# Attention inside two mixed layers: row sums and norms issued behind the products with V, and a unit's additions placed behind the low part of a projection sum on VectorE

## The chip, the cores and the metric

The kernel runs on one core of a Trainium2 chip. The metric is the device time of one launch in microseconds (us). Three runs of the kernel before took 3855.62, 3857.41 and 3857.58 us, so the median is 3857.41 us.

## The reference

Four residual steps are computed on a sequence of 2048 rows with 1024 columns: attention, a spectral filter, attention, the spectral filter, each on the layer-normed input. The change touches attention alone, which has 32 heads of 32 columns.

```python
def _A_ref(x, wqkv, wo):
    B, S, D = x.shape
    H = 32
    Dh = D // H
    qkv = (lambda x, *d: x.transpose(*d))((x @ wqkv).reshape(B, S, 3, H, Dh), 2, 0, 3, 1, 4)
    q, k, v = qkv[0], qkv[1], qkv[2]
    scores = jnp.einsum("bhqd,bhkd->bhqk", q, k) * (Dh ** -0.5)
    p = _softmax(scores, axis=-1)
    o = jnp.einsum("bhqk,bhkd->bhqd", p, v)
    return (lambda x, *d: x.transpose(*d))(o, 0, 2, 1, 3).reshape(B, S, D) @ wo
...
x = A_x
x = x + _A_ref(_layernorm(x, axis=-1), A_wqkv, A_wo)
x = x + _B_ref(_layernorm(x, axis=-1), B_w_r, B_w_i)
x = x + _A_ref(_layernorm(x, axis=-1), A_wqkv, A_wo)
x = x + _B_ref(_layernorm(x, axis=-1), B_w_r, B_w_i)
```

## The kernel before

**Units.** Attention works on 8 groups `g` of 4 heads. In a group the 2048 query rows are cut into 4 chunks `c` of 512, and the 2048 keys into 16 tiles `kt` of 128. One step of the main loop, a *unit* (g, c, kt), is one key tile against one chunk of queries, so a layer has 512 units. The text writes S(n), add(n) and so on for key tile n of a chunk.

**What a unit issues.** `S` (L557) makes the scores: 12 TensorE matmuls (L563) that use 32 rows of the array each, into two PSUM tiles `s` of 1024 columns, followed by two exponentials on ScalarE (L567), which write the halves of `p`. `PV` (L569) multiplies `p` with V: matmuls in fp32 that use 32 columns of the array each (L573). They are issued for two units at once, at each even key tile. `add` (L580) adds the two halves of `p` into two running sums `acc` on VectorE, two instructions (L586; L584 at key tile 1, which adds the tiles 0 and 1). At key tile 0 there is nothing to add.

**Row sums.** After the last key tile of a chunk, `fin` (L588) sums `acc` over the partitions: four fp32 matmuls with a 128x32 block of ones (L592), 32 array columns each as in `PV`. Their output `z` takes a PSUM tile of the same pool as the scores (`psS`, 3 tiles in turn). VectorE transposes `z` (L593), inverts it (L595), and multiplies the product with V (L596 to L599). At key tile 5 of that next chunk `out` (L602) splits the result in a high and a low half: L605 on ScalarE, L606 on VectorE.

**The filler.** Behind the scores of each odd key tile, TensorE gets a piece of the next groups' projections (`filler`, L397, portioned by `slots`, L619). A projection sum for k or q (`qk_chunk`, L324) is 24 matmuls into a single PSUM tile `x` (`psX`, one buffer), portioned as 8+8+8 or 12+12. When it is done, `split` (L165) reads `x` twice: ScalarE writes the high fp16 part (L167), then VectorE the low part (L168), which needs the high one. The next sum's first matmul needs `x` back, that is, the low part done. VectorE also squares the high part (`sq`, L342). A group with even `g` has 12 such sums beside it (4 for each of k, q, k), a group with odd `g` 4 (q) and then 8 sums for v, which ScalarE alone empties; group 6 has 8 and then pieces of the output projection, group 7 only those. The projection weights of the next phase are split as well, by L167 and L168 on tiles `wqk` and `wv`; in the first layer alone, VectorE also takes their maxima (L259).

**Norms.** After the fourth sum of a k or q phase, `norms` (L349) sums the squares over each head: four bf16 matmuls with a 128x32 block (L355), 32 columns each, into a tile of `psS` again, which VectorE reduces to a maximum (L357, `mqk`). In the main loop there are 14 of these in a layer.

**What sets the order.** On TensorE and ScalarE the main loop's own order holds (`manual_schedule`, L633). On VectorE a scheduler places instructions by the program's order and by when it takes their inputs to be ready, when the kernel is built; on the chip each engine then works its list in that fixed order. At an even key tile n the loop issues S(n), the products of the units n-2 and n-1, and add(n-2); at the odd tile n+1 it issues S(n+1), add(n-1), and then the filler. The row sums stand at key tile 1 of the next chunk, behind add(15), and norms stand in `slots`, ahead of a filler piece.

## Time and profile before

| what | value |
|---|---|
| median of three runs | 3857.41 us |
| profiled execution, its own time | 3855.25 us |
| profiled execution, span of the trace | 3853.3 us |
| TensorE matmuls busy | 3720.5 us, 97% |
| VectorE busy | 3165.8 us, 82% |
| ScalarE busy | 2898.3 us, 75% |
| granted TensorE clock, mean | 0.99 |
| main attention loop, first layer (first to last scores) | 123.5 to 1624.1 us |
| main attention loop, second layer | 2046.8 to 3535.6 us |

The profile's page has the busy time of each engine, the chain of work that ended last, and the costliest groups of instructions. A group's row reads: line, engine, operation, out<-in, shapes, count, then busy time, mean of one in ns, and the idle time of the engine just before such instructions with what ended it. The timeline's rows read: start in us from the span's start, length in us, engine, line, operation, out<-in, shapes, count; equal neighbours are merged into one row, and in brackets stands the idle time ahead with what released it. The ends of matmuls are modelled, so that the text takes the cost of a group of matmuls from its start to the start of the next group.

### The profile page before, as it was taken

To read this page: it belongs to the slowest core of one execution; us is meant where nothing else is said; L and a number is where in the kernel's file an instruction comes from. 1 tells how busy PE (TensorE), PEld (TensorE's weight loads), DVE (VectorE), ACT (ScalarE), POOL (GpSimd) and SP (SyncE) were. 2 spreads that over 40 slices of the span, in tenths; PEclk is the share of its full clock that TensorE was granted. 3 is DMA by queue.
4 is the path that set the end of the run, shared out by engine and by line. 5 is a ranking of instruction groups with operands and counts; after the bars stand their busy time and mean duration, and the time that the engine had idled before them with its cause. 6 is when DMAs were issued, how large, how long until landed. Compare 5 with 4: busy or idle time off the path is not lost.

```text
span 3853.3 us, 79584 instructions
## 1 busy us (share of the span) xinstructions
PE 3720.5 (97%) x32951; PEld 1640.1 (43%) x32951; DVE 3165.8 (82%) x3869; ACT 2898.3 (75%) x3567; POOL 303.0 (8%) x386
## 2 busy tenths in 40 slices
PE   6999999999999999999989999999999999999998
PEld 4322433342234233378853334333423432333788
DVE  6699899889998988866666998899899889889554
ACT  4678887888788866667756888888888888666585
POOL 1000000000000000004320000000000000000143
PEclk9999999999999999999999999999999999999999
DMA  8000000000000221243270000000000002112433
GB/s 206 15 12 23 12 12 18 18 12 18 12 26 7 73 71 64 80 149 124 63 175 15 18 18 13 12 18 23 10 18 12 23 12 91 53 64 72 150 99 104
DMA packets 165573, 194.07 MB, mean 50 GB/s; under 512 B 74960, under 2 KB 120656, under 8 KB 164176
## 3 DMA queue, kind: packets, MB, share of 16 engines
q1 hardware_dynamic: 164912, 188.82, 15.9%
q8 instruction: 260, 4.26, 0.5%
q14 instruction: 113, 0.93, 0.1%
q10 hardware_dynamic: 288, 0.07, 0.0%
HBM read 123.83 MB, written 48.23 MB: 45 GB/s over the span
## 4 chain that ended last, share of the span: by engine, by line
PE 73%; DVE 12%; issue 8%; ACT 3%; DMA 2%; POOL 2%; SPq 0%; DVEq 0%; POOLq 0%; ACTq 0%
PE o L573 19%; PE s L563 16%; PE x L338 12%; PE x L382 7%; PE x L441 6%; DVE R L586 4%; PE s L441 2%; PE ps L861 2%; PE ps L801 2%; ACT p L567 1%; PE s L592 1%; PE ps L792 1%; DMA wst<-in_wp 1%; PE ps L976 1%; PE ps L930 1%
## 5 line engine op out<-in xcount | busy, mean ns | idle before, releaser
L567 ACT ACTIVATE p<-s,bias 128x1024 f32<-128x1024 f32 x2048 | 2167.8, 1111 | 553.5 <-PE s L563 542.6
L586 DVE TENSOR_TENSOR R<-R,p 128x1024 f32<-128x1024 f32 x1792 | 2085.4, 1219 | 111.2 <-ACT p L567 107.8
L573 PE MATMUL o<-p,R 128*32 128x512 f32 x8192 | 985.0, 598 | 0.0
L338 PE MATMUL x<-big,wqk 128*128 128x512 f16 x2880 | 682.7, 383 | 21.1 <-DVE Q L168 6.5
L563 PEld LDWEIGHTS <-R 32*128 32x128 f16 x12288 | 231.6, 92 | 760.3 <-issue 644.6
L338 PEld LDWEIGHTS <-wqk 128*128 128x128 f16 x3072 | 277.6, 98 | 458.5 <-issue 165.4
L563 PE MATMUL s<-R 32*128 32x512 f16 x6144 | 430.9, 378 | 10.6 <-ACT p L567 8.9
L573 PEld LDWEIGHTS o<-p,R 128*32 128x32 f32 x8192 | 213.7, 109 | 523.8 <-issue 523.8
L563 PE MATMUL s<-Q,R 32*128 32x512 f16 x6144 | 425.4, 378 | 7.5 <-DVE R L482 5.5
L382 PEld LDWEIGHTS <-big 128*128 128x128 f16 x3072 | 293.1, 99 | 144.3 <-issue 66.2
L382 PE MATMUL x<-wv,big 128*128 128x256 f16 x2688 | 320.5, 275 | 35.0 <-DMA big<-hl 35.0
L584 DVE SCALAR_TENSOR_TENSOR R<-p 128x1024 f32<-128x1024 f32 x128 | 153.8, 1203 | 198.9 <-ACT p L567 198.6
L441 PE MATMUL x<-big 128*128 128x512 f16 x1050 | 241.6, 380 | 0.0
L363 POOL PARTITION_ALL_REDUCE mall<-mqk x16 | 41.8, 2612 | 2325.5 <-DVE mqk L357 2313.9
L441 PEld LDWEIGHTS <-big 128*128 128x128 f16 x1344 | 124.3, 98 | 180.5 <-issue 42.7
L909 DVE TENSOR_TENSOR H<-G,H 128x512 f16<-128x512 f32 (+1 forms) x68 | 46.3, 680 | 113.1 <-ACT H L908 112.9
L861 PE MATMUL ps<-cbi,H 128*128 128x256 f16 (+1 forms) x792 | 100.5, 275 | 7.9 <-ACT H L908 6.2
L854 ACT COPY U<-ps 64x256 f32<-64x256 f32 (+1 forms) x272 | 97.0, 357 | 11.6 <-PE ps L861 6.4
L854 ACT COPY B<-ps 64x256 f32<-64x256 f32 (+1 forms) x272 | 97.0, 356 | 7.0 <-PE ps L861 2.8
L861 PE MATMUL ps<-cb,big 128*128 128x256 f16 x780 | 97.6, 275 | 0.0
L167 ACT ACTIVATE R<-x 128x512 f16<-128x512 f32 x88 | 52.6, 598 | 54.8 <-PE x L338 54.7
L806 DVE TENSOR_TENSOR big<-ps,big 128x512 f16<-128x512 f32 x64 | 44.4, 694 | 50.4 <-ACT big L805 50.3
(428 smaller groups left out, 2967.7 us busy)
## 6 DMA issues: line engine op xcount, KB each, us to landing
wst<-in_wp SPq DMA_DIRECT2D x96, 256.0 KB, 3.0
R<-y SPq DMA_DIRECT2D x32, 512.0 KB, 5.4
w<-in_w SPq DMA_DIRECT2D x60, 256.0 KB, 2.7
od<-ohl SPq DMA_DIRECT2D x56, 256.0 KB, 2.4
big<-od SPq DMA_DIRECT2D x16, 896.0 KB, 7.0
y<-R SPq DMA_DIRECT2D x20, 512.0 KB, 2.6
R<-in_x SPq DMA_DIRECT2D x16, 512.0 KB, 5.6
wst<-in_wo SPq DMA_DIRECT2D x32, 256.0 KB, 3.0
```

The source lines that it names most:

```text
L167: nc.scalar.activation(hi, src, AF.Copy, scale=scale)
L338: nc.tensor.matmul(ps, a, b, start=d == 0 and i == 0, stop=d == 7 and i == 2)
L382: nc.tensor.matmul(ps[:, j], l, r, start=d == 0 and i == 0, stop=d == 7 and i == 2)
L441: nc.tensor.matmul(p, a, b, start=start and d == ds[0] and i == 0, stop=stop and d == ds[-1] and i == 2)
L563: nc.tensor.matmul(s[h // 2][:, h % 2], K[g][r, a, kt * 128:kt * 128 + 128], Q[g][r, b, c * 512:c * 512 + 512], start=i == 0, stop=i == 2)
L567: nc.scalar.activation(p, s[hf], AF.Exp, bias=bias[g], scale=SCALE / (SQ * SQ))
L573: nc.tensor.matmul(O[g, c][32 * h:32 * h + 32], V[g][:, kt, 32 * h:32 * h + 32], P[g, c, kt, h // 2][:, h % 2], start=kt == 0, stop=kt == ...
L584: nc.vector.scalar_tensor_tensor(acc[hf], P[g, c, 0, hf], 1e-34, p, op0=ALU.add, op1=ALU.add)
L586: nc.vector.tensor_add(acc[hf], acc[hf], p)
L801: nc.tensor.matmul(pa[:, j], tt[:, j], mm[:, g], start=True, stop=True)
L854: nc.scalar.copy(ov[64 * r:64 * r + 64, a0:a0 + m, x], tl[64 * x:64 * x + 64, :m, r])
L861: nc.tensor.matmul(out, l, r, start=k == 0, stop=k == len(mm_) - 1)
```

## The change

Three things are moved; no instruction is added, removed or made otherwise.

1. At key tile 0 of a chunk, the loop issues the additions of both of the last units (tiles 14 and 15 of the chunk before) and the row sums `fin` at once, directly behind the products with V. `fin` stood one unit later, behind the scores of key tile 1.
2. `norms` is taken out of `slots`. It is called at key tiles 2, 6, 10 and 14, directly behind the products with V.
3. `split` returns the instruction of the low part, and `qk_chunk` keeps it in a list `lows`. At an odd key tile, if `lows` holds one, the additions of the pair's second unit are traced inside `tc.issue_after(...)`: on VectorE they must stand behind that low part. The low part is that of the sum that ended two units earlier, at the key tile of the very unit that is added.

```diff
@@ -1,5 +1,5 @@
 import numpy as np
-from contextlib import ExitStack
+from contextlib import ExitStack, nullcontext
 import concourse.bass as bass
 import concourse.tile as tile
 from concourse import mybir
@@ -165,7 +165,7 @@
 def split(nc, hi, lo, src, scale):
 
     nc.scalar.activation(hi, src, AF.Copy, scale=scale)
-    nc.vector.scalar_tensor_tensor(lo, src, scale, hi, op0=ALU.mult, op1=ALU.subtract)
+    return nc.vector.scalar_tensor_tensor(lo, src, scale, hi, op0=ALU.mult, op1=ALU.subtract)
 
 
 def run(g):
@@ -338,13 +338,13 @@
                 nc.tensor.matmul(ps, a, b, start=d == 0 and i == 0, stop=d == 7 and i == 2)
                 if d < 7 or i < 2:
                     yield
-        split(nc, t[:, 0], t[:, 1], ps, SQ / (SX * SW))
+        lows.append(split(nc, t[:, 0], t[:, 1], ps, SQ / (SX * SW)))
         (nc.gpsimd if both else nc.vector).tensor_tensor(nrm[ph][:, c], t[:, 0], t[:, 0], op=ALU.mult)
         if c == 3:
             left_norms.append(ph)
         yield
 
-    left_norms = []
+    left_norms, lows = [], []
 
     def norms():
         kind, g = ph = left_norms.pop(0)
@@ -609,6 +609,7 @@
         else:
             olast[c] = t
 
+    lows.clear()
     pend, done, late = [], [], []
     fill, lwo, wof = filler(), load_wo(), wo_parts()
     left, rests = 16, {}
@@ -622,8 +623,6 @@
             k = max(1, int(n / sums + 0.5))
             m = -(-steps // k)
             for i in range(0, steps, m):
-                while left_norms:
-                    norms()
                 for _ in range(min(m, steps - i)):
                     next(f, None)
                 n -= 1
@@ -643,11 +642,18 @@
                         PV(*w)
                     late = pend
                     pend = []
+                    if kt == 0 and late:
+                        for w in late:
+                            add(*w)
+                        done = [late[1][:2]]
+                        fin(*done[0])
+                        late = []
+                if kt % 4 == 2:
+                    while left_norms:
+                        norms()
                 for w in late[:1]:
-                    add(*w)
-                    if w[2] == NKT - 1:
-                        fin(*w[:2])
-                        done = [w[:2]]
+                    with tc.issue_after(lows.pop().ins) if kt % 2 and lows else nullcontext():
+                        add(*w)
                 late = late[1:]
                 if kt == 5 and done:
                     out(*done.pop())
```

The lists of TensorE, VectorE and the others that result are these. ScalarE, GpSimd and the DMA queue keep their order.

On VectorE, second layer, group 2, end of chunk 0. `L586` x2 is the additions of one unit, `R<-x,R` of L168 the low part of a projection sum, `sq` the square, `wqk` the low part of weights, L593 the transpose of the row sums. Before:

```order
L168 SCALAR_TENSOR_TENSOR R<-x,R 128x512
L342 TENSOR_TENSOR sq<-R 128x512
L586 TENSOR_TENSOR R<-R,p 128x1024 x12
L168 SCALAR_TENSOR_TENSOR R<-x,R 128x512
L342 TENSOR_TENSOR sq<-R 128x512
L586 TENSOR_TENSOR R<-R,p 128x1024 x4
L168 SCALAR_TENSOR_TENSOR wqk<-wst,wqk 128x512 x2
L586 TENSOR_TENSOR R<-R,p 128x1024 x4
L584 SCALAR_TENSOR_TENSOR R<-p 128x1024
L593 STREAM_TRANSPOSE zt<-s 128x512
L584 SCALAR_TENSOR_TENSOR R<-p 128x1024
```

With the change:

```order
L168 SCALAR_TENSOR_TENSOR R<-x,R 128x512
L342 TENSOR_TENSOR sq<-R 128x512
L586 TENSOR_TENSOR R<-R,p 128x1024 x12
L168 SCALAR_TENSOR_TENSOR R<-x,R 128x512
L342 TENSOR_TENSOR sq<-R 128x512
L586 TENSOR_TENSOR R<-R,p 128x1024 x6
L168 SCALAR_TENSOR_TENSOR wqk<-wst,wqk 128x512 x2
L586 TENSOR_TENSOR R<-R,p 128x1024 x4
L593 STREAM_TRANSPOSE zt<-s 128x512
L595 RECIPROCAL rc<-zt 128x16
L596 TENSOR_TENSOR fr<-fr,rc 128x16
```

The second low part has moved ahead of the additions of one unit: of those, x6 instead of x4 now stand between it and the weights' low parts. The additions of the sum's own key tile are behind it. The row sums' chain now stands ahead of L584, the next chunk's first additions, not among them.

On TensorE, second layer, the row sums of the same chunk (with the semaphores that an instruction waits for). Before, behind the last scores of key tile 1 and ahead of the filler:

```order
L563 MATMUL s<-R 128x512
L592 MATMUL s<-R,ones 32x512 [waits DVE_49,Activation_49]
L592 MATMUL s<-R,ones 32x512
L592 MATMUL s<-R,ones 32x512 [waits DVE_49]
L592 MATMUL s<-R,ones 32x512
L338 LDWEIGHTS wqk
L338 MATMUL x<-big,wqk 128x512
```

With the change, behind the products with V and ahead of the scores of key tile 1:

```order
L573 MATMUL o<-p,R 32x512 x6
L573 MATMUL o<-p,R 32x512 [waits Activation_49]
L573 MATMUL o<-p,R 32x512
L592 MATMUL s<-R,ones 32x512 [waits DVE_49,PE_49]
L592 MATMUL s<-R,ones 32x512
L592 MATMUL s<-R,ones 32x512 [waits DVE_49]
L592 MATMUL s<-R,ones 32x512
L563 LDWEIGHTS R
L563 MATMUL s<-R 128x512 [waits Activation_49]
```

The first of the row sums waits for the additions to the first half of `acc`, the third for those to the second half, now with one unit's scores less ahead of them.

On VectorE, the maximum of a norm (L357) in chunk 1 of the same group. Before, behind the additions of key tile 8:

```order
L586 TENSOR_TENSOR R<-R,p 128x1024 x4
L168 SCALAR_TENSOR_TENSOR R<-x,R 128x512
L342 TENSOR_TENSOR sq<-R 128x512
L586 TENSOR_TENSOR R<-R,p 128x1024 x2
L357 TENSOR_REDUCE mqk<-s 128x1
L586 TENSOR_TENSOR R<-R,p 128x1024 x10
```

With the change, behind the additions of key tile 10:

```order
L586 TENSOR_TENSOR R<-R,p 128x1024 x2
L168 SCALAR_TENSOR_TENSOR R<-x,R 128x512
L342 TENSOR_TENSOR sq<-R 128x512
L586 TENSOR_TENSOR R<-R,p 128x1024 x8
L357 TENSOR_REDUCE mqk<-s 128x1
L586 TENSOR_TENSOR R<-R,p 128x1024 x4
```

The norm's matmuls stood at key tile 9 behind the scores, and now stand at key tile 10 behind the products.

## The prediction

> **What bounds the kernel now.** I read the page's shares first, then the two main loops as stretches, then the timeline of one chunk's end. TensorE is the bound.
>
> ```profile
> PE 3720.5 (97%) x32951; PEld 1640.1 (43%) x32951; DVE 3165.8 (82%) x3869; ACT 2898.3 (75%) x3567; POOL 303.0 (8%) x386
> 123.50:1624.10 1500.60, 1473.78 (x13578) 508.66 (x13576) 1348.54 (x1427) 1180.98 (x1246) 32.30 (x28) 1.00 0.08 28
> 2046.80:3535.60 1488.80, 1472.24 (x13577) 508.04 (x13576) 1324.76 (x1390) 1180.83 (x1246) 28.79 (x28) 1.00 0.09 28
> L338 PE MATMUL x<-big,wqk 128*128 128x512 f16 x2880 | 682.7, 383 | 21.1 <-DVE Q L168 6.5 <-DVE R L168 6.2 <-ACT wqk L167 5.4
> L584 DVE SCALAR_TENSOR_TENSOR R<-p 128x1024 f32<-128x1024 f32 x128 | 153.8, 1203 | 198.9 <-ACT p L567 198.6 <-PE s L592 0.3
> ```
>
> In the loops TensorE is idle for 1500.6 - 1473.8 = 26.8 us and 1488.8 - 1472.2 = 16.6 us. From start to start, which is the measure used below, waits are larger, since the rows' ends are modelled. VectorE stands free for 152.1 and 164.0 us, some 10%. So VectorE costs nothing as long as what waits for it has slack, and the question is where that slack is. The row of L338 shows one place where it ends before: 12.7 us on low parts (6.5 and 6.2). The row of L584 shows where VectorE's own free time lies: it waits some 3 us per chunk for the next chunk's first `p`.
>
> The timeline of the second layer, group 2, shows the end of chunk 0 on all three engines (weight loads left out):
>
> ```profile
> 2430.43 11.50 DVE L586 TENSOR_TENSOR R<-R,p 128x1024 f32<-128x1024 f32 x10
> 2437.55 0.83 PE L563 MATMUL s<-R 32*128 32x512 f16 x12
> 2438.31 1.92 PE L573 MATMUL o<-p,R 128*32 128x512 f32 x16
> 2440.17 0.82 PE L563 MATMUL s<-R 32*128 32x512 f16 x12
> 2440.93 1.90 PE L338 MATMUL x<-big,wqk 128*128 128x512 f16 x8
> 2441.03 2.12 ACT L567 ACTIVATE p<-s,bias 128x1024 f32<-128x1024 f32 x2 [0.49 <-PE s L563]
> 2442.18 2.36 DVE L586 TENSOR_TENSOR R<-R,p 128x1024 f32<-128x1024 f32 x2 [0.25 <-ACT p L567]
> 2442.76 0.83 PE L563 MATMUL s<-R 32*128 32x512 f16 x12
> 2443.04 0.60 ACT L167 ACTIVATE R<-x 128x512 f16<-128x512 f32 x1
> 2444.45 0.68 DVE L168 SCALAR_TENSOR_TENSOR R<-x,R 128x512 f16<-128x512 f32 x1
> 2445.39 4.63 DVE L586 TENSOR_TENSOR R<-R,p 128x1024 f32<-128x1024 f32 x4
> 2449.93 1.29 DVE L168 SCALAR_TENSOR_TENSOR wqk<-wst,wqk 128x512 f16<-128x512 f32 x2
> 2451.13 4.62 DVE L586 TENSOR_TENSOR R<-R,p 128x1024 f32<-128x1024 f32 x4
> 2455.78 0.83 PE L563 MATMUL s<-R 32*128 32x512 f16 x12
> 2456.54 1.06 PE L592 MATMUL s<-R,ones 128*32 128x512 f32 x8
> 2457.54 1.90 PE L338 MATMUL x<-big,wqk 128*128 128x512 f16 x8
> ...
> 2494.93 2.76 PE L338 MATMUL x<-big,wqk 128*128 128x512 f16 x12
> 2497.63 0.83 PE L563 MATMUL s<-R 32*128 32x512 f16 x12
> ```
>
> A pair of units costs TensorE 2442.76 - 2437.55 = 5.21 us: scores 0.76, two products 1.86, scores 0.76, eight filler matmuls 1.83. VectorE needs 4.63 us for the pair's four additions, so it regains about 0.29 us per unit when it is late. A projection sum ends with the filler at 2440.93; ScalarE's high part follows the unit's exponentials and is done at 2443.64; VectorE meanwhile adds the same unit (2442.18 to 2444.54) and then takes the low part and the square in 2445.39 - 2444.45 = 0.94 us.
>
> **The change part by part.**
>
> *Row sums behind the products.* Twelve filler matmuls take 2497.63 - 2494.93 = 2.70 us and eight 1.83, so 512 columns stream in 0.22 us. The row sums are four fp32 matmuls side by side, in four passes: 0.87 us of streaming. They cost 2457.54 - 2456.54 = 1.00, so 0.13 us goes to the change of the array's shape. Behind the products, which have their shape, that should go: 62 chunk ends inside the loops, -0.13 each, -8 us. Bounds: 0 (the cost stays) and -9.
> The row is first; the Trainium skill, TensorEngine Tiling (Array Packing), Key Properties, says that a change of tiling mode drains the engine, and the same shape follows itself without it. By that rule alone the sum would be -8 for row sums and -3 for norms. The trace agrees in size, by the 0.13.
>
> *Norms behind the products.* The same saving would be 0.33 - 0.22 = 0.11 us each, 28 times, -3 (rows below). But the norm now takes the third `s` tile, so the next scores need the tile of the unit just begun, whose exponentials end about 0.15 us after TensorE gets there: scores begun at 2440.17 are through their exponentials at 2441.03 + 2.12, 2.98 us on, and TensorE comes 0.76 + 1.86 + 0.22 = 2.84 us on. I take 0, bounds -3 and +3.
>
> *The low part ahead of its unit's additions.* This is the term that decides. Here add(10) ends at 2430.43 + 11.50 = 2441.93. The next on VectorE's list is then the low part, which has to wait for 2443.64, idle 1.7 us although add(11) could start at 2442.18. With 0.94 us for low part and square, add(11) starts near 2444.64 and ends at 2447.0, where the unit after it began at 2445.39 before. So all that is queued behind is 1.5 to 1.6 us later: add(12), add(13), the weights' low parts, add(14), add(15). In this stretch VectorE had no pause from 2445.39 to 2455.75 that could absorb it. add(15) now ends at 2457.3. The row sums, no longer behind the scores of key tile 1, are reached at 2455.78, and their second half, 0.43 us later, waits for just that: 2457.3 - 2456.2 = 1.1 us of TensorE, where it waited for nothing before. Chunk 0 ends like this in groups 0 to 6 of the second layer and in group 6 of the first: 8 x 1.1 = 9 us. In groups 0 to 5 of the first layer VectorE also takes weight maxima there:
>
> ```profile
> 536.42 2.35 DVE L586 TENSOR_TENSOR R<-R,p 128x1024 f32<-128x1024 f32 x2
> 537.22 0.83 PE L563 MATMUL s<-R 32*128 32x512 f16 x12
> 537.98 1.90 PE L592 MATMUL s<-R,ones 128*32 128x512 f32 x8
> 539.81 1.90 PE L338 MATMUL x<-big,wqk 128*128 128x512 f16 x8
> ```
>
> There add(15) ends at 538.77, and the row sums already lost 1.83 - 1.00 = 0.83 us. With 1.3 us more on VectorE (the lower side of the above, since the maxima may have pauses that absorb a little) it ends at 540.1, where TensorE would want it at 537.22 + 0.43: 2.4 us, 1.6 more than before, x6 = 10 us. Together +19. Bounds: 0, if the additions end in time after all, and twice that, if chunks 1 and 2 of the even groups, which end with smaller backlogs, pay too.
> The Trainium skill says the same of the mechanism in PSUM — Partial Sum Buffer, Engine vs sequencer instructions: queues of VectorE and ScalarE are strictly first in, first out, which speaks against this edit. The trace agrees, in another stretch of the same loop, where VectorE has nothing but a low part ahead and stands until ScalarE's high part is done, idle for 1.26 us:
>
> ```profile
> 3260.51 0.69 DVE L168 SCALAR_TENSOR_TENSOR Q<-x,Q 128x512 f16<-128x512 f32 x1 [1.26 <-ACT Q L167]
> ```
>
> *Where the norm's maximum stands.* The tile that the norm took comes back when VectorE has taken its maximum, and the second scores after it need it.
>
> ```profile
> 2475.26 0.60 ACT L167 ACTIVATE R<-x 128x512 f16<-128x512 f32 x1
> 2478.36 0.40 PE L355 MATMUL s<-sq,bones 128*32 128x512 bf16 x4
> 2478.69 1.90 PE L338 MATMUL x<-big,wqk 128*128 128x512 f16 x8
> 2480.41 0.69 DVE L357 TENSOR_REDUCE mqk<-s 128x1 f32<-128x512 f32 x1
> 2480.52 0.39 PE L563 MATMUL s<-R 32*128 32x512 f16 x2
> 2481.15 0.82 PE L563 MATMUL s<-R 32*128 32x512 f16 x10 [0.24 <-DVE mqk L357]
> ...
> L355 PE MATMUL s<-sq,bones 128*32 128x512 bf16 x128 | 15.4, 387 | 9.4 <-DVE sq L342 6.9 <-ACT p L567 1.6 <-POOL sq L342 1.0
> ```
>
> Before, the maximum is among the next instructions: scores 0.63 us late (2480.52 to 2481.15). With the change: low part of key tile 7 at 2475.9, add(7) from 2476.85, four units of 2.315 us, add(10) ends at 2486.1, maximum at 2486.8. TensorE, with the norm's 0.33 gone from its old place, begins key tile 10 at 2480.19, and one pair (5.21), the norm behind the products (0.22) and the wait for exponentials (0.15) later key tile 12, at 2485.77: it waits 1.05 us. At key tile 14 (chunk 2 of even groups) the same working gives 0.9; in odd groups, with two more low parts of V's weights (1.29 us by the row at 2449.93), 2.2; in the first layer with the maxima 2.8, where the low part itself is late by 0.65, and 1.25 in chunk 2. At key tile 2 nothing. A layer has three even and odd pairs of groups, and group 6 with 2: 3 x (1.05 + 0.9 + 2.2) + 2 = 14 and 3 x (1.05 + 1.25 + 3.45) + 2 = 19, 33 us in all. Before, norms waited for squares (6.9 of the 9.4 us in the row of L355) and held scores and filler up as above; all such waits sum to 21 us from start to start, over the 28 norms. In their place: +12. Bounds: -21 (none waits) and +25.
>
> *Low parts that were late.* They are now one unit earlier. The largest cost 2.01 us:
>
> ```profile
> 602.21 4.63 DVE L586 TENSOR_TENSOR R<-R,p 128x1024 f32<-128x1024 f32 x4
> 604.66 0.83 PE L563 MATMUL s<-R 32*128 32x512 f16 x12
> 606.75 0.68 DVE L168 SCALAR_TENSOR_TENSOR Q<-x,Q 128x512 f16<-128x512 f32 x1
> 607.49 2.75 PE L338 MATMUL x<-big,wqk 128*128 128x512 f16 x12 [2.01 <-DVE Q L168]
> ```
>
> Four additions stood ahead of it from 602.21 on, of which two go behind. Of the 12.7 us I take -8: in groups 0 to 5, 9 us go and about 1 stays; those of group 6 have weights' low parts waiting for DMA around them and stay. Bounds 0 and -12.7.
>
> *Hidden edits.* The transpose and inverse of the row sums now run ahead of the next chunk's first additions. The wait for the first `p` (L584) hides them. Their price without that cover: two transposes of 0.71 us and three shorter instructions, about 2.2 us of backlog per chunk.
>
> ```profile
> L593 DVE STREAM_TRANSPOSE zt<-s 128x512 f32<-128x512 f32 x64 | 45.4, 709 | 0.0
> ```
>
>
> Sum: -8 + 0 + 19 + 12 - 8 = **+15 us**, against the profiled execution's 3855.25. The median stands 2.2 above that execution, so 3857.4 + 15 = 3872, and I round to 3873 for the group 6 ends (weights' low parts now ahead of add(13), about 0.5 each).
>
> **The rivals.**
>
> *The backlog never reaches TensorE: faster.* The row sums' chain leaves the middle of the additions, and VectorE has 152 and 164 us free. If it is never late where chunks end or maxima are due, the terms +19 and +12 become 0 and up to -21, the row sums' waits of the first layer go as well (6 x about 1 us), and what is left is -8 - 8 and some 10 to 20 of those: about 3828. It decides at add(15): it must end at most 0.43 us after TensorE leaves the products of key tile 15. For it: in the sample add(15) kept that bound before, with 2455.75 against 2455.78. Against: the sample, where two or three low parts per chunk each cost VectorE up to 1.7 us, and a regain of 0.29 per unit.
>
> *The pieces cancel: no difference.* With the bounds halfway (chunk ends +10, maxima +5) the sum is -1: 3857. For it: four terms of similar size with both signs.
>
> *VectorE becomes the bound: much slower.* Some 39 low parts per layer move ahead of additions within a chunk (8 in each even group, 3 in each odd one, 6 in group 6). If each idles 1.5 us, 117 us of the 316 free ones go; chunk ends 1 and 2 of even groups and the first layer's maxima then pay 1 to 3 us each as well, some +35: 3892. Against: a VectorE that is late already has the high part ready, so the idle time limits itself.
>
> *It doesn't do what it says.* VectorE's list shows the moves; only a low part that came first anyway, such as at key tile 15, is moved past nothing.
>
> **How the numbers follow.** A measurement of this kernel tells about 0.2%, 7.7 us, from no change. My forecast (+8 to +25) has 0.50, much slower 0.15, cancelled 0.20, faster 0.15. So slower 0.65, within 0.2% 0.20, faster 0.15. The likeliest case alone spans 3865 to 3883. The range reaches to part of the others: up to 3897 (the third rival), down to 3845, which leaves out most of the faster case and little else.
>
> **What would show it.** Right: in the second layer the row sums (L592) of chunk 0 stretch from 0.87 to about 2 us, with a wait for L586; scores two units after a norm wait for L357 about 1 us; VectorE idles 1 to 1.7 us before L168, released by L167; filler matmuls (L338) no longer wait for L168 in groups 0 to 5. Row sums that start where the products end and cost 0.87 confirm the first term. Wrong: additions of key tile 15 that end with the products, or no idle time ahead of L168; then the faster rival holds.

## The result, and the profile after

Four runs of the changed kernel took 3885.09 to 3888.37 us, median 3887.52. Four runs of the kernel before, on the same chip, took 3851.55 to 3857.58, median 3856.51. The ratio is 1.0079, with a 95% interval of 1.0067 to 1.0091. The kernel became slower, by some 30 us; the forecast was 15, with 8 to 25 as its likeliest case. The profiled execution took 3885.09 us, 29.8 more than that of before.

The two main loops as stretches come first, from the first scores to the last, as total, then TensorE, weight loads, VectorE, ScalarE and GpSimd busy:

```profile
123.93:1640.76 1516.83, 1475.62 (x13579) 513.66 (x13579) 1355.27 (x1427) 1180.27 (x1246) 38.04 (x28) 1.00 0.08 28
2064.19:3565.90 1501.71, 1476.01 (x13577) 513.28 (x13577) 1331.87 (x1390) 1180.27 (x1246) 37.81 (x28) 1.00 0.08 28
```

The loops are 16.3 us (1516.83 - 1500.53, from the first scores of the first layer on) and 12.9 us (1501.71 - 1488.86) longer. All but some 0.7 us of the profiled execution's loss lies in them. TensorE has no more work than before (the counts are the same to one or two records), the granted clock is 1.00 as it was, so the loss is waiting.

Of the groups of instructions of the kernel after, these rows answer to the prediction's: busy time, mean, then idle time ahead and what ended it.

```profile
L338 PE MATMUL x<-big,wqk 128*128 128x512 f16 x2880 | 682.4, 382 | 14.8 <-ACT wqk L167 5.4 <-DVE R L168 4.7 <-DVE Q L168 1.8
L563 PE MATMUL s<-R 32*128 32x512 f16 x6144 | 432.5, 379 | 24.3 <-DVE mqk L357 13.9 <-ACT p L567 10.4
L563 PE MATMUL s<-Q,R 32*128 32x512 f16 x6144 | 425.5, 377 | 14.5 <-DVE mqk L357 11.8 <-DVE R L482 2.6
L592 PE MATMUL s<-R,ones 128*32 128x512 f32 x512 | 85.8, 596 | 16.7 <-DVE R L586 13.8 <-DVE R L482 2.9
L168 DVE SCALAR_TENSOR_TENSOR R<-x,R 128x512 f16<-128x512 f32 x88 | 60.5, 688 | 45.8 <-ACT R L167 45.8
L168 DVE SCALAR_TENSOR_TENSOR Q<-x,Q 128x512 f16<-128x512 f32 x32 | 22.0, 689 | 34.0 <-ACT Q L167 33.6
L606 DVE TENSOR_TENSOR ohl<-zt,ohl 128x512 f16<-128x512 f32 x64 | 43.8, 685 | 29.6 <-ACT ohl L605 29.6
```

The same view of the kernel before has, for six of them:

```profile
L563 PE MATMUL s<-R 32*128 32x512 f16 x6144 | 430.9, 378 | 10.6 <-ACT p L567 8.9 <-DVE mqk L357 1.6
L563 PE MATMUL s<-Q,R 32*128 32x512 f16 x6144 | 425.4, 378 | 7.5 <-DVE R L482 5.5 <-DVE mqk L357 1.9
L592 PE MATMUL s<-R,ones 128*32 128x512 f32 x512 | 72.9, 604 | 1.4 <-DVE R L586 1.4
L168 DVE SCALAR_TENSOR_TENSOR R<-x,R 128x512 f16<-128x512 f32 x88 | 59.3, 674 | 19.7 <-ACT R L167 19.7
L168 DVE SCALAR_TENSOR_TENSOR Q<-x,Q 128x512 f16<-128x512 f32 x32 | 21.6, 676 | 1.3 <-ACT Q L167 1.3
L606 DVE TENSOR_TENSOR ohl<-zt,ohl 128x512 f16<-128x512 f32 x64 | 43.8, 685 | 0.0
```

Read from the bottom up, the rows tell the story. VectorE now stands idle ahead of low parts, until ScalarE's high part is done: 45.8 + 34.0 us, where it was 19.7 + 1.3. It also stands ahead of L606, the low part of a chunk's output, 29.6 us where it was nothing. The change never names that instruction, but it stands in VectorE's list just ahead of a low part and came forward with it. Together 109.4 us of idle time in front of a ScalarE result, 88 more than before. What TensorE waits for, then, is VectorE: additions (L586) ahead of row sums, 13.8 us for 1.4, and maxima (L357) ahead of scores, 25.7 us for 3.5. Only the filler (L338) waits less for low parts, 6.5 us for 12.7.

The timeline of the second layer, group 2, chunk 0, shows how one such idle time becomes a loss. First its beginning, at key tile 5, VectorE and ScalarE alone:

```profile
2444.46 2.36 DVE L586 TENSOR_TENSOR R<-R,p 128x1024 f32<-128x1024 f32 x2 [0.23 <-ACT p L567]
2446.26 2.12 ACT L567 ACTIVATE p<-s,bias 128x1024 f32<-128x1024 f32 x2 [0.83 <-PE s L563]
2448.27 0.62 ACT L605 CAST ohl<-zt 128x512 f16<-128x512 f32 x1
2448.78 0.61 ACT L167 ACTIVATE R<-x 128x512 f16<-128x512 f32 x1
2448.92 0.69 DVE L606 TENSOR_TENSOR ohl<-zt,ohl 128x512 f16<-128x512 f32 x1 [2.10 <-ACT ohl L605]
2449.53 0.68 DVE L168 SCALAR_TENSOR_TENSOR R<-x,R 128x512 f16<-128x512 f32 x1
...
2450.46 13.71 DVE L586 TENSOR_TENSOR R<-R,p 128x1024 f32<-128x1024 f32 x12
...
2464.35 0.69 DVE L168 SCALAR_TENSOR_TENSOR R<-x,R 128x512 f16<-128x512 f32 x1 [0.18 <-ACT R L167]
```

VectorE is free at 2446.82 and stands for 2.10 us, until ScalarE has cast the output; the low part, next in the list, could not have started before 2449.39 either. The exponentials of this unit run from 2446.26 to 2448.38, so its first addition could have started near 2447.4, and starts at 2450.46. Six units of additions follow without a pause. At the second low part VectorE idles 0.18 us only: being late itself, it finds the high part done. The lateness is kept, not doubled. The end of the chunk, VectorE and TensorE:

```profile
2473.30 4.62 DVE L586 TENSOR_TENSOR R<-R,p 128x1024 f32<-128x1024 f32 x4
...
2474.60 1.92 PE L573 MATMUL o<-p,R 128*32 128x512 f32 x16
...
2476.94 2.10 PE L592 MATMUL s<-R,ones 128*32 128x512 f32 x8 [0.41 <-DVE R L586]
2477.98 0.14 PEld L592 LDWEIGHTS s<-R,ones 128*32 128x32 f32 x4 [0.90 <-DVE R L586]
2478.97 0.83 PE L563 MATMUL s<-R 32*128 32x512 f16 x12
```

add(15) ends at 2477.92. The products, undisturbed, free TensorE 1.86 us from their start, at 2476.46. The row sums start 0.48 us later, their second half waits again until 2477.98, and the next scores start at 2478.97: 1.64 us behind what 1.86 + 0.86 would give. The prediction took 1.1 for it.

A second place is the norm in chunk 1 of the same group, by the same view:

```profile
2503.14 1.92 PE L573 MATMUL o<-p,R 128*32 128x512 f32 x16
2504.88 0.40 PE L355 MATMUL s<-sq,bones 128*32 128x512 bf16 x4
2505.21 1.02 PE L563 MATMUL s<-R 32*128 32x512 f16 x12
2506.17 1.90 PE L338 MATMUL x<-big,wqk 128*128 128x512 f16 x8
2508.11 0.68 DVE L357 TENSOR_REDUCE mqk<-s 128x1 f32<-128x512 f32 x1
2508.84 0.83 PE L563 MATMUL s<-R 32*128 32x512 f16 x12 [0.77 <-DVE mqk L357]
```

The matmuls of the norm end near 2505.3, but VectorE takes the maximum at 2508.11, behind additions. The scores start at 2508.84 where 2506.17 + 1.83 = 2508.00 was possible. Ahead of it is the small price of the norm's new place: scores take 2506.17 - 2505.21 = 0.96 us instead of 0.76, for exponentials that still read the tile.

**One account for all kernels.** For each group of TensorE instructions in the two loops I took the time from its start to the next start, less what the same group costs undisturbed (scores 0.76 us, products 1.86, eight filler matmuls 1.83, row sums 0.86, norm 0.22). What is over, in us, sorted by what stands there:

| kernel | row sums | norms and their maxima | filler late | rest | both loops |
|---|---|---|---|---|---|
| before | 16.3 | 24.0 | 21.7 | 19.4 | 2989.4 |
| after | 38.5 | 28.7 | 25.5 | 17.9 | 3018.5 |
| low parts alone | 29.6 | 54.4 | 14.3 | 26.8 | 3033.0 |
| rows and norms alone | 14.8 | 3.7 | 31.9 | 17.0 | 2975.3 |
| rows alone | 14.9 | 26.3 | 17.6 | 15.8 | 2982.5 |
| norms alone | 14.1 | 8.0 | 33.8 | 20.6 | 2984.4 |
| rows, low parts | 39.1 | 54.7 | 15.1 | 22.7 | 3039.6 |
| norms, low parts | 28.0 | 30.6 | 22.8 | 23.2 | 3012.5 |
| all, low part between | 19.5 | 10.4 | 21.5 | 16.3 | 2975.7 |
| low part between, alone | 17.1 | 31.4 | 15.6 | 19.3 | 2991.4 |
| after, low parts in chunks 1 to 3 only | 20.5 | 30.6 | 25.3 | 20.0 | 3004.4 |
| after, low parts in chunk 0 only | 35.3 | 7.1 | 31.3 | 16.6 | 2998.3 |
| the faster version | 12.9 | 6.8 | 21.7 | 16.1 | 2965.4 |

Of the 16.3 us of before, 8.4 are the change of the array's shape, 62 x 0.135. The other kernels are those of the experiments. The loops and the row sums' column follow from the starts alone. Which wait belongs in which of the three columns between depends on the sorting: another one, by what released each wait, moves several us between them (21.1 and 27.2 us for the norms of the first two kernels, 17.5 for rows alone). Where norms stand behind the products, the filler's column holds one thing more: the scores behind each norm last 0.20 us longer, as in the last timeline, 28 x 0.203 = 5.7 us.

### The profile page after: what moved, and what is told of

Read it like the earlier page. It is cut to its first block, busy times and chain, and to the rows that moved or that the text cites. A ratio compares the mean times of both kernels' runs of the same rounds, so it can differ in the third digit from the quotient of the medians.

```text
span 3883.2 us, 79442 instructions
## 1 busy us (share of the span) xinstructions
PE 3726.0 (96%) x32951; PEld 1651.3 (43%) x32951; DVE 3179.3 (82%) x3869; ACT 2897.3 (75%) x3567; POOL 318.3 (8%) x386
## 3 DMA queue, kind: packets, MB, share of 16 engines
q1 hardware_dynamic: 164912, 188.82, 15.8%
## 5 line engine op out<-in xcount | busy, mean ns | idle before, releaser
L586 DVE TENSOR_TENSOR R<-R,p 128x1024 f32<-128x1024 f32 x1792 | 2076.3, 1217 | 98.9 <-ACT p L567 97.1
L338 PE MATMUL x<-big,wqk 128*128 128x512 f16 x2880 | 682.4, 382 | 14.8 <-ACT wqk L167 5.4
L338 PEld LDWEIGHTS <-wqk 128*128 128x128 f16 x3072 | 276.6, 98 | 440.3 <-issue 145.9
L382 PE MATMUL x<-wv,big 128*128 128x256 f16 x2688 | 320.5, 275 | 38.4 <-DMA big<-hl 35.3
L382 PEld LDWEIGHTS <-big 128*128 128x128 f16 x3072 | 293.6, 99 | 135.7 <-issue 57.5
L584 DVE SCALAR_TENSOR_TENSOR R<-p 128x1024 f32<-128x1024 f32 x128 | 150.7, 1218 | 36.9 <-ACT p L567 36.9
L593 DVE STREAM_TRANSPOSE zt<-s 128x512 f32<-128x512 f32 x64 | 45.7, 715 | 94.6 <-PE s L592 94.6
L860 ACT COPY U<-ps 64x256 f32<-64x256 f32 (+1 forms) x272 | 97.2, 357 | 11.7 <-PE ps L867 6.6
L592 PE MATMUL s<-R,ones 128*32 128x512 f32 x512 | 85.8, 596 | 16.7 <-DVE R L586 13.8
L168 DVE SCALAR_TENSOR_TENSOR R<-x,R 128x512 f16<-128x512 f32 x88 | 60.5, 688 | 45.8 <-ACT R L167 45.8
```

The lines of the kernel that those rows point to most:

```text
L168: return nc.vector.scalar_tensor_tensor(lo, src, scale, hi, op0=ALU.mult, op1=ALU.subtract)
L338: nc.tensor.matmul(ps, a, b, start=d == 0 and i == 0, stop=d == 7 and i == 2)
L382: nc.tensor.matmul(ps[:, j], l, r, start=d == 0 and i == 0, stop=d == 7 and i == 2)
L584: nc.vector.scalar_tensor_tensor(acc[hf], P[g, c, 0, hf], 1e-34, p, op0=ALU.add, op1=ALU.add)
L586: nc.vector.tensor_add(acc[hf], acc[hf], p)
L592: nc.tensor.matmul(z[32 * h:32 * h + 32], cst["ones"], acc[h // 2][:, h % 2], start=True, stop=True)
```

## The experiments

The change has three parts: row sums behind the products ("rows"), norms behind the products ("norms"), and a unit's additions behind the low part ("low parts"). **Theory A**: the wait that the third part forces on VectorE makes the loss, and the other two save time by themselves. **Theory B**, the rival: the two moves on TensorE take a unit of slack from VectorE and make the loss, while the low part's place gains. The first six kernels hold the other combinations of the three parts. Each was run beside the kernel before.

**Low parts alone.**

```diff
-        split(nc, t[:, 0], t[:, 1], ps, SQ / (SX * SW))
+        lows.append(split(nc, t[:, 0], t[:, 1], ps, SQ / (SX * SW)))
...
-                    add(*w)
+                    with tc.issue_after(lows.pop().ins) if kt % 2 and kt > 1 and lows else nullcontext():
+                        add(*w)
```

> Only the low part of the projection sum is put ahead of the additions of its own unit (from key tile 2 on); row sums stay behind the scores of key tile 1, norms at odd key tiles. Theory A (VectorE's forced wait for the high part makes a backlog of some 2.5 us, and the two moves on TensorE only meet it): the backlog is there as in the full change, but row sums have one unit's scores (0.76 us) more before they are due: chunk ends +10 to +12 us over both layers instead of +31, low parts -4, waits of norms for squares about -8, so 3846 to 3867 us, near 3856. Theory B (the two moves take away a unit of slack and cost by themselves, the low part's place is harmless): the late low parts alone go, -8 us, 3848 us, and VectorE shows no additions later than 2 us behind their exponentials at chunk ends.

Measured: 3894.37 us, ratio 1.0103 (1.0088 to 1.0119). That is slower than the whole change, so B falls: the third part alone costs 38 us. A's figure, 3856, was wrong too, by the norms. Their column in the account is 54.4 for 24.0 before, where I had counted on 8 us less. The scores' rows of this kernel name the cause:

```profile
L563 PE MATMUL s<-R 32*128 32x512 f16 x6144 | 434.7, 379 | 29.9 <-DVE mqk L357 19.8 <-ACT p L567 10.0
L563 PE MATMUL s<-Q,R 32*128 32x512 f16 x6144 | 427.2, 379 | 18.8 <-DVE mqk L357 13.3 <-DVE R L482 5.5
```

Scores wait 33.1 us for maxima, before 3.5 us. At its old place, at an odd key tile, a norm's tile is needed back by the very next scores, and the maximum stands behind the late additions. The timeline of TensorE and VectorE shows one such case:

```profile
2508.42 0.39 PE L563 MATMUL s<-R 32*128 32x512 f16 x2
2509.27 0.68 DVE L357 TENSOR_REDUCE mqk<-s 128x1 f32<-128x512 f32 x1
...
2510.01 0.82 PE L563 MATMUL s<-R 32*128 32x512 f16 x10 [1.20 <-DVE mqk L357]
```

The chunk ends came out near the expectation: 29.6 - 16.3 = 13 us, expected 10 to 12. From here on theory A reads: the backlog makes late whatever stands behind it on VectorE and is due within a unit or two.

**Rows and norms alone.**

```diff
-                while left_norms:
-                    norms()
...
+                    if kt == 0 and late:
+                        for w in late:
+                            add(*w)
+                        done = [late[1][:2]]
+                        fin(*done[0])
+                        late = []
+                if kt % 4 == 2:
+                    while left_norms:
+                        norms()
...
-                    if w[2] == NKT - 1:
-                        fin(*w[:2])
-                        done = [w[:2]]
```

> Row sums and norms stand behind the products, but VectorE's additions keep the order of the kernel before. Theory A: no backlog is made, so what is left are the savings: row sums' change of shape -8.6 us, norms' change of shape -3.2 us, waits around norms -13 us, and +4 us for chunk 0 of the first layer, whose row sums were late already: about 3836 us (3830 to 3842). Theory B: the loss of a unit's slack costs by itself, chunk ends and maxima are late as in the full change: 3872 us or more.

Measured: 3844.35 us, ratio 0.9974 (0.9964 to 0.9984). Faster than before: the two moves need no cover from the third part. The 8 us that A was short of are in the filler's column, 31.9 for 21.7. Of the 10 more, 5.7 are the longer scores behind norms, for which this expectation had no term. The rest is mainly waits for low parts, 20 us where 12.7 were, by the rows of this kernel (L338 and L382 are filler):

```profile
L338 PE MATMUL x<-big,wqk 128*128 128x512 f16 x2880 | 682.0, 382 | 20.7 <-DVE R L168 6.9 <-DVE Q L168 5.6 <-ACT wqk L167 5.4
L382 PE MATMUL x<-wv,big 128*128 128x256 f16 x2688 | 323.1, 277 | 42.5 <-DMA big<-hl 35.1 <-DVE R L168 7.4
```

L338 waits as before; the rise is L382, the first sum for V in odd groups. Before, the norm stood ahead of that filler and waited there itself, for the square that VectorE makes right behind this low part (the 6.9 us in the row of L355). With the norm elsewhere, the filler meets the wait. So a part of the waits around norms, which A had as a gain, only changed its name.

**Rows alone** and **norms alone** are the halves of that diff: its first six added lines (up to `late = []`, with the old call of `fin` taken out), or the lines with `norms`.

> Only the row sums stand behind the products; norms and the order of additions are those of the kernel before. Theory A: -8.6 us for the change of shape, +4 us for chunk 0 of groups 0 to 5 in the first layer, where the row sums were already late by 0.83 us: about 3852 us, within 3848 to 3857. Theory B: the row sums wait about 1.5 us at the end of chunk 0 of nearly all groups and some at others: +20 us less the 8.6, 3868 us.

> Only the norms stand behind the products of even key tiles; row sums and the order of additions are those of the kernel before. Theory A: the norms' change of shape -3.2 us and the waits around them -13 us, less about 4 us (0.15 to 0.2 each) for exponentials at the following scores: 3840 to 3847 us, and the maximum stands behind fewer late additions, so scores wait for L357 less than 5 us in all. Theory B: the maximum is late by itself, scores wait some 27 us for L357 as in the full change: 3865 to 3870 us.

Measured: rows 3851.25 us, ratio 0.9985 (0.9976 to 0.9994); norms 3848.95, ratio 0.998 (0.9971 to 0.9989). Rows fit A. Norms are 2 us above its bound, again by late fillers (33.8 in the account): L382 waits 8.0 us for low parts here, and not at all with rows alone. The gains are near 0.2%, but both intervals lie below 1, and B's 3865 to 3870 is out of reach.

**Rows with low parts, norms with low parts** are the whole change without `norms` moved, or without `fin` moved.

> Row sums behind the products and the low part ahead, norms at their old places. Theory A (refined: the backlog makes late whatever stands behind it and is due within a unit): maxima of norms at odd key tiles are as late as with the low part alone (scores of the next key tile wait some 44 us in all), and row sums as in the full change, some 9 us more than with the low part alone: about 3903 us (3897 to 3908), the slowest of all. Theory B (row sums behind products gain or lose by themselves): 3894 less the 5.4 us that rows alone gained, 3889 us.

> Norms behind the products and the low part ahead, row sums at their old place with one unit's scores more before they are due. Theory A (refined): the maxima have a pair of units more than at odd key tiles, which takes back some 20 to 25 us of the 38 that the low part alone costs, and the chunk ends stay as with the low part alone: 3869 to 3879 us, faster than the full change by 9 us or more. Theory B: norms alone gained 7.7 us and would gain the same here: 3886 us.

Measured: 3905.26 us, ratio 1.0131 (1.0115 to 1.0146), and 3880.36, ratio 1.0066 (1.0052 to 1.008). The first is what the refined theory said, and the slowest of all. The second is 1.4 us above its bound, but below B's 3886. With both of them each part's worth can be read in both surroundings, as differences of medians: rows alone gain 5 us, and cost 11 when low parts stand ahead (3905.3 - 3894.4). Norms gain 8 alone, 14 with low parts, 18 with low parts and rows (3887.5 - 3905.3). Low parts cost 38 alone, 54 with rows, 31 with norms, 43 with both. So rows behind products are a good move made bad, norms behind products are the part that limits the damage, and the low part is the damage in every company.

**What of the low part costs?** Its 0.94 us with the square must be spent in any case. The next kernel puts it between its unit's two additions: the first can run while ScalarE makes the high part, so VectorE need not idle, but one addition still stands behind. Against the whole change:

```diff
-    def add(g, c, kt):
+    def add(g, c, kt, low=None):
         for hf in range(2):
             p = P[g, c, kt, hf]
-            if kt == 1:
+            with tc.issue_after(low.ins) if hf and low else nullcontext():
+                if kt == 1:
...
-                    with tc.issue_after(lows.pop().ins) if kt % 2 and lows else nullcontext():
-                        add(*w)
+                    add(*w, low=lows.pop() if kt % 2 and lows else None)
```

> Row sums and norms behind the products as in the full change, but the low part stands between the two additions of its unit: only the second addition is queued behind it, so it comes 1.2 us later than in the full change, when ScalarE's high part is done to within some 0.3 us. Theory A (what costs is VectorE's idle wait for the high part): VectorE's idle time ahead of low parts falls from 46 us to under 25 us, chunk ends and maxima cost about what they do with rows and norms alone (15 and 3 us), fillers wait for low parts some 5 to 10 us less: 3834 to 3844 us. Rival C (what costs is that additions stand behind the low part's 0.94 us at all, with or without an idle wait): row sums and maxima stay late by most of what they are in the full change, 3860 us or more.

> Nothing but the low part's place changes, and it stands between the two additions of its unit. Theory A: without the idle wait the 38 us that the low part alone costs go almost wholly; left are half a unit's later maxima, so 3848 to 3862 us. Rival C: the additions behind the low part are late in any case: 3875 us or more.

Measured: 3842.74 us, ratio 0.9965 (0.9951 to 0.9978), for the whole change with the low part between. 3859.84, ratio 1.001 (1.0001 to 1.0019), with nothing but the low part between. Against the low part ahead of both additions that is 44.8 and 34.5 us less, for one addition of 1.2 us that now goes first. (L606 stands right ahead of the low part in both lists and moves with it.) Rival C falls as the main cause. It may hold for what is left: row sums and maxima keep 19.5 - 14.8 = 4.7 and 10.4 - 3.7 = 6.7 us over rows and norms alone, where the whole change has 23.7 and 25.0. The rows of the first of the two (additions are L587 here):

```profile
L592 PE MATMUL s<-R,ones 128*32 128x512 f32 x512 | 77.2, 594 | 7.9 <-DVE R L587 5.0 <-DVE R L482 2.9
L168 DVE SCALAR_TENSOR_TENSOR R<-x,R 128x512 f16<-128x512 f32 x88 | 60.4, 687 | 24.2 <-ACT R L167 23.6
L168 DVE SCALAR_TENSOR_TENSOR Q<-x,Q 128x512 f16<-128x512 f32 x32 | 22.1, 690 | 10.1 <-ACT Q L167 9.7
L606 DVE TENSOR_TENSOR ohl<-zt,ohl 128x512 f16<-128x512 f32 x64 | 43.9, 686 | 5.2 <-ACT ohl L605 5.2
```

VectorE's idle time ahead of these three falls from 109.4 to 39.5 us. The timeline of VectorE and ScalarE at the second low part of the same chunk:

```profile
2436.63 0.60 ACT L167 ACTIVATE R<-x 128x512 f16<-128x512 f32 x1
2437.22 2.12 ACT L567 ACTIVATE p<-s,bias 128x1024 f32<-128x1024 f32 x2
2437.26 0.69 DVE L168 SCALAR_TENSOR_TENSOR R<-x,R 128x512 f16<-128x512 f32 x1 [0.27 <-ACT R L167]
...
2438.20 5.76 DVE L587 TENSOR_TENSOR R<-R,p 128x1024 f32<-128x1024 f32 x5
```

It waits 0.27 us, and the additions go on.

**Where it falls.** Does the lateness of one chunk reach the next? Two kernels split the whole change by chunks; the first has `if low and c`, the second `if low and c == 0`:

```diff
-                    with tc.issue_after(lows.pop().ins) if kt % 2 and lows else nullcontext():
+                    low = lows.pop() if kt % 2 and lows else None
+                    with tc.issue_after(low.ins) if low and c else nullcontext():
```

> The full change, but in chunk 0 of every group low parts keep the place they had before; ahead of their unit they stand in chunks 1 to 3 only. Theory A (a backlog lasts some units and is gone at a chunk's start, so its cost falls where it was made): row sums at the end of chunk 0 cost what they do with rows and norms alone, some 18 us less than in the full change, less 1 to 3 us of late low parts that come back, and scores still wait some 28 us for L357: 3870 us (3865 to 3875). Rival D (backlogs are carried on through a group): the time stays within 8 us of the full change, or falls to that of rows and norms alone.

> The mirror of it: low parts stand ahead of their unit in chunk 0 of every group only, and keep their place in chunks 1 to 3. Theory A: only the row sums at the end of chunk 0 are late, by 1.5 us in the second layer, and scores wait under 6 us in all for L357: rows and norms alone (3844) + 18 = 3862 us (3857 to 3867). With the run beside it the two parts add up to what the full change loses against rows and norms alone (43 us). Rival D: under 3850 us, or near the full change.

Measured: 3874.19 us, ratio 1.0046 (1.0033 to 1.006), and 3865.55, ratio 1.0025 (1.0016 to 1.0034). Their rows of scores and row sums, of the first and then of the second:

```profile
L563 PE MATMUL s<-R 32*128 32x512 f16 x6144 | 431.8, 378 | 24.8 <-DVE mqk L357 13.9 <-ACT p L567 10.9
L592 PE MATMUL s<-R,ones 128*32 128x512 f32 x512 | 78.7, 596 | 5.9 <-DVE R L586 2.9 <-DVE R L482 2.9
```

```profile
L563 PE MATMUL s<-R 32*128 32x512 f16 x6144 | 431.2, 378 | 7.2 <-ACT p L567 6.9 <-DVE mqk L357 0.2
L592 PE MATMUL s<-R,ones 128*32 128x512 f32 x512 | 82.2, 598 | 17.1 <-DVE R L586 14.2 <-DVE R L482 2.9
```

Late maxima come from chunks 1 to 3, late row sums from chunk 0, each without the other: both times lie within theory A's bounds, and outside what rival D gave. Over rows and norms alone the two cost 29.8 and 21.2 us by their medians, 51 together, where the whole change costs 43.2 over the same kernel. The parts very nearly add up; with intervals of some 5 us each, I leave the 8 open.

**A faster version.** The stretches show that the two layers want different things: with the low part between, the first layer's loop took 1494.7 us, 4.0 less than rows and norms alone, the second's 1481.0, 4.4 more. And in the first layer row sums at the end of chunk 0 are late even with rows and norms alone, by 10.5 us over groups 0 to 5. Against the whole change with the low part between:

```diff
-                    if kt == 0 and late:
+                    if kt == 0 and late and (layer or c != 1):
...
-                    add(*w, low=lows.pop() if kt % 2 and lows else None)
+                    add(*w, low=lows.pop() if kt % 2 and kt > 1 and lows and not layer else None)
+                    if w[2] == NKT - 1:
+                        fin(*w[:2])
+                        done = [w[:2]]
```

> For a faster kernel: norms behind the products; row sums behind them too, but for the end of chunk 0 in the first layer, where they are late and stand behind one unit's scores as before; low parts between the two additions of their unit in the first layer, and at their old place in the second. From the stretches of the runs so far: 3842.7 us of the kernel with low parts between, less 4.4 us (second layer as with rows and norms alone), less some 5 us (6 row sums in the first layer): 3833 us (3829 to 3839). If the waits only move on, 3840 to 3844 us.

Measured: 3836.88 us (3830.35 to 3841.56), ratio 0.9952 (0.9939 to 0.9966): 0.5% faster than before, and the fastest of these kernels, though its interval touches those of rows and norms alone and of the low part between.

## Why the prediction was right, and where its sizes were off

The direction, the place and the mechanism held: VectorE idles ahead of a high part, additions queue behind, and row sums and maxima meet the backlog. The size was half. The measured time lies above the +8 to +25 us of the likeliest case, and in the range only because that was drawn up to the third rival: that it lies there is in part luck. Term by term, with what the account gives between before and after (a us or so depends on the sorting):

| term | predicted | measured |
|---|---|---|
| row sums, change of shape | -8 | -8.4 |
| norms: shape, and exponentials behind them | -3 + 3 | -3.2 + 5.7 |
| row sums wait at chunk ends | +19 | +30.5 |
| maximum at its new place | +12 | +7.9 |
| low parts that were late | -8 | -2.4 |
| rest of the loops, and outside | 0 | -0.4 |
| sum | +15 | +29.7 |

**Row sums' shape.** Right to half a us. Products and row sums together took 1.86 + 1.00 = 2.86 us and take 2.72 where nothing is late. Most of the saving shows in the products, 1.74; the row sums take 0.98, not the 0.87 that I had named as the sign.

**Row sums at chunk ends**: this is the step that was mis-sized, by 11.5 us. In chunk 0 of the second layer I had add(15) 1.1 us late, taking "their second half, 0.43 us later" as the time by which it is due. The additions came 1.46 us after the products' end in the timeline above, and TensorE lost 1.64. The 0.43 was the error. The four matmuls run side by side in four strips of the array, so two take as long as four: after add(15), 0.86 us is still to come, plus the start. The Trainium skill, TensorEngine Tiling (Array Packing), Key Properties, says that tiles work independently and in parallel, and the trace agrees: the weights of the second half at 2477.98, the next scores at 2478.97, 0.99 us on, when all four matmuls take 1.00. Eight such ends cost 13.1 us, for 9 predicted. In groups 0 to 5 of the first layer the ends cost 11.7 us more than before, for 10. The other 6 or so (less 1.1 saved at chunk 3) had no term: chunk 1 of group 6, 1.1 us twice, chunk 1 of even groups, 0.2 to 0.3, and chunk 1 of group 7, 1.6 us twice. The last has another cause, VectorE's sum for the output projection (L482), and rows and norms alone pay it too.

One end of the first layer, group 3, shows how far the backlog had grown there:

```profile
726.52 2.35 DVE L586 TENSOR_TENSOR R<-R,p 128x1024 f32<-128x1024 f32 x2
727.88 2.10 PE L592 MATMUL s<-R,ones 128*32 128x512 f32 x8 [2.03 <-DVE R L586]
728.92 0.14 PEld L592 LDWEIGHTS s<-R,ones 128*32 128x32 f32 x4 [0.90 <-DVE R L586]
729.91 0.83 PE L563 MATMUL s<-Q,R 32*128 32x512 f16 x12
```

**The maximum.** The waits that vanish were 20.4 us, forecast 21. Those that come are 28.3, forecast 33: 0.84 and 0.66 us in even groups of the second layer (forecast 1.05 and 0.9), 1.55 in odd ones (2.2), 2.5 in odd ones of the first layer (3.45). Each forecast was a little too long; why, I did not follow up. Group 6 was the other way, 3.0 us per layer (0.84 + 2.14) for 2.

**Exponentials behind norms.** I had 0.15 us for each; they take 0.20 at most norms, and the 0.12 of shape does not pay for them.

**Late low parts.** The waits of filler for them in groups 0 to 5 fell from 9.0 us, as the prediction had it, but to 5.4 and not to 1: three new ones, 3.1 us by the rows, stand ahead of the first sum for V in odd groups of the first layer. The rows of that sum, of the kernel before, of the whole change and of low parts alone:

```profile
L382 PE MATMUL x<-wv,big 128*128 128x256 f16 x2688 | 320.5, 275 | 35.0 <-DMA big<-hl 35.0
L382 PE MATMUL x<-wv,big 128*128 128x256 f16 x2688 | 320.5, 275 | 38.4 <-DMA big<-hl 35.3 <-DVE R L168 3.1
L382 PE MATMUL x<-wv,big 128*128 128x256 f16 x2688 | 320.1, 275 | 35.2 <-DMA big<-hl 35.2
```

The moved norm is what uncovers them, as with rows and norms alone: the wait is in every kernel with norms behind the products (2.8 to 8.0 us) and in none with norms at their old place. There, with low parts ahead, the waits of groups 0 to 5 did fall to 1.4 us (low parts alone) and 1.6 (rows, low parts). The term itself was right, then; what it missed is that the norm had covered a wait. Those around group 6 grew from 10.7 to 12.0.

**The forced wait itself.** The price, 1.5 us of lateness per chunk, was right, but not where I put it. I saw it made by the second low part of the chunk. It is made by the first, by L606 ahead of it as well, and the second then waits 0.18. That an engine which is late waits no more, which I held against the third rival, is what these two rows show; but it bounds less than I thought. VectorE regains the lateness within a chunk and can wait again: 1.44 and 1.29 us at two low parts of chunk 2 of the same group. Of the 117 us of idle time that the third rival set down, 88 came.

The rivals: the backlog did reach TensorE, the pieces did not cancel, and VectorE did not become the bound of whole stretches: it stands free for 1516.83 - 1355.27 = 161.6 us in the first loop and 169.8 in the second, no less than before. The measured 3887.5 lies nearer to the third rival's 3892 than to the forecast. Of its mechanism, three quarters of the idle time came, but not the waits that it added: chunks 1 and 2 of even groups pay 0.3 us or nothing for row sums, where it had 1 to 3, and the first layer's maxima stayed below the forecast's.

## What to carry to other kernels

An instruction that waits for another engine should not be queued ahead of work that is ready: here one addition of 1.2 us, put ahead of such an instruction instead of behind it, was worth 35 to 45 us. Where an order is forced on a list that a scheduler fills, look at what else comes forward with the instruction (here the output's low part), and take apart a change of several parts before it is kept or dropped: two of these three parts gain, and one of the two gains only while the third is absent. When an instruction that waits is moved away, look at what stood behind it: the wait may pass to that. A result that is due half an operation later than its partner is not due later at all if the halves run side by side, as the four matmuls here.

## What the runs showed of the hardware

Products and row sums have the same shape in fp32, and the norm has it in bf16. The norm behind the products started 2504.88 - 2503.14 = 1.74 us after them, as the row sums, of the same type, do where nothing is late (1.74, against 1.86 ahead of another shape). So the change of type between matmuls of one shape cost nothing that these starts show, and a change of shape 0.12 to 0.14 us (1.86 - 1.74, and 2.86 - 2.72 for products and row sums).
